# Dummy TensorE instructions ahead of three steps of the first batch

## The chip, the cores and the metric

The kernel runs on one core of a Trainium2 chip. The metric is device time in microseconds (us). A core has five engines that work side by side and wait for each other through semaphores: TensorE (PE in the profile, its weight loads are PEld), VectorE (DVE), ScalarE (ACT), GpSimd (POOL) and SyncE (SP, which here only issues DMAs). PSUM is the memory that TensorE writes its results into; DVE and ACT copy them from there to SBUF.

## What is computed

A cosformer attention without a softmax (features are a relu, weighted by a cosine and a sine of the position) is followed by an MLP mixer, with 8 batches, 8 heads, 576 positions and head dimension 64:

```python
def phi(x, c, s):
    r = np.maximum(x, 0.0)
    return np.concatenate([r * c, r * s], axis=-1)
q_p = phi(q, cos_w, sin_w)
k_p = phi(k, cos_w, sin_w)
kv = np.einsum('bhsf,bhsd->bhfd', k_p, v)
z = np.sum(k_p, axis=2)
num = np.einsum('bhsf,bhfd->bhsd', q_p, kv)
den = np.einsum('bhsf,bhf->bhs', q_p, z)[..., None] + 1e-06
x = num / den                     # heads side by side: (8, 576, 512)
...
xt = x.transpose(0, 2, 1)
h = np.maximum(xt @ w_tok1, 0.0) @ w_tok2
u = x + h.transpose(0, 2, 1)
h2 = np.maximum(u @ w_ch1, 0.0) @ w_ch2
return u + h2
```

## The kernel before

All 576 positions of a batch lie as five groups of rows on 128 partitions (index j from 0 to 4; P5 in the code pairs them as (0, 1), (2, 3) and (4,)). Heads come in two halves g = 0 and 1 of four heads each; g = 2 means all eight. The products are bf16 with sums in f32.

The order of the first two batches, and of part of the third and fourth, is written out as the string PLAN: each word is one step, called in that order, so that each engine receives its instructions in the order of the words. `turn.0.0.1` means batch 0, method `turn`, arguments 0 and 1. Engines run ahead of each other as far as the semaphores let them. From batch 2 on the loop `channel` runs the channel MLP of one batch with the attention of the next as hooks in between.

The steps of the first batch that the change and the prediction touch:

- `keep_warm` (L188 to L191) comes first on TensorE: 20 products of the zero tile with itself into a PSUM tile `wm`.
- `mkid` makes the 128x128 identity `ident` on GpSimd (masks.py in the trace).
- `feat` (L293) makes the features qp and kp from the loaded q and k, one group of rows, one half (cosine or sine) at a time, on ACT (L300) or DVE (L302).
- `cast` (L304) copies v to bf16 (`vbf`); the words that end in P run on GpSimd, whose queue also issues weight loads (`wt1`, `wt2`, `wu`, `wd`) and q of the second batch (`ldp`).
- `turn` (L309) transposes qp on TensorE, four heads for each group of rows, into a bf16 PSUM tile `tr`; `turno` copies that to `qpT` on ACT or DVE (L263, the line of all copies).
- `kvm` (L337) sums kp times v over the five groups into a PSUM tile `kv`, 20 products of 128x65 for one half of the heads; `kvo` copies it to SBUF.
- `num` (L368) multiplies qpT by kv, `numo` divides and writes `x` (DVE, L381 and L387).
- `w2a` copies the second token weights into their place (ACT, L263).
- `mix` (L403) multiplies the first token weights by x, into the PSUM tile `b1`.

Two PSUM pools serve them: psM, four slots of one bank, and psA, two slots of two banks. In the first batch `tr`, the kv tiles of half the heads and `b1` of half the heads are in psM. A step that takes a slot waits until the slot's last user is done with it.

A transpose and a product are both MATMUL instructions in the trace, each with a weight load of its own; L315 is the transposes' line, L331 that of the kv products, L361 and L365 those of num, L410 that of mix.

## Time and profile before

| | |
|---|---|
| median of 4 runs | 276.33 us (276.04 to 277.12) |
| profiled execution, its own time | 277.12 us |
| its span in the trace | 275.4 us, 4673 instructions |
| TensorE busy | 260.2 us, 94% of the span |
| DVE, ACT, POOL busy | 170.8, 116.5, 54.0 us |
| mean granted TensorE clock | 0.988 |
| idle TensorE ahead of the first transposes (L315, at 12.38 us) | 3.60 us, released by DVE qp |
| idle TensorE ahead of the next 24 (at 15.98 us) | 3.20 us, released by ACT qp |
| idle TensorE ahead of the first mix product (L410, at 22.01 us) | 1.12 us, released by DVE x |

The profile gives, for every instruction, its start and duration, and what ended the idle time of its engine before it. The granted clock is the share of TensorE's full clock that the chip allowed at that moment. Durations of matmuls are modelled and overlap, so the rate of a group is read from the starts of neighbouring groups. The chain that ended last is followed backwards from the last instruction, at each step to what released it, and shows which work set the end.

### The profile page before, as it was taken

The page shows a single profiled execution, that of the slowest core. Times are in us where ns is not written, and L with a number is a line of the kernel's source. Part 1 is how long each engine was busy: PE and PEld are TensorE (multiplying, and loading weights), DVE is VectorE, ACT ScalarE, POOL GpSimd, SP SyncE. Part 2 cuts the span into 40 slices and gives each one's busy share as a digit, 9 for nine tenths or more (in the row PEclk, how much of TensorE's full clock was granted, in tenths as well). Part 3 has the DMA queues.
Part 4 walks back from the last instruction along what each step waited for, and adds up shares of the span by engine and source line. Part 5 has one row for each costly group of instructions (what it writes and reads, how often), then busy time and mean ns, then how long its engine had stood idle before and what let it go on. Part 6 is the DMA issues. An engine that isn't in the chain of part 4 may idle for free.

```text
span 275.4 us, 4673 instructions
## 1 busy us (share of the span) xinstructions
PE 260.2 (94%) x1846; PEld 134.2 (49%) x1846; DVE 170.8 (62%) x338; ACT 116.5 (42%) x185; POOL 54.0 (20%) x76
## 2 busy tenths in 40 slices
PE   6367999999999999999999999999999999999994
PEld 2166556445544554454445544554455444444443
DVE  6467897599783476947584859485738543323322
ACT  2388684473790339133822482248224201301300
POOL 9580150051030005410160017001100120000000
PEclk9959999999999999999999999999999999999999
DMA  5999999999899999999999878930990073003012
GB/s 186 344 253 222 326 161 265 368 327 173 270 200 233 288 366 369 178 197 267 360 191 255 279 249 110 228 105 1 154 258 11 0 115 135 0 14 141 0 45 108
DMA packets 76005, 53.35 MB, mean 194 GB/s; under 512 B 47824, under 2 KB 72400, under 8 KB 75984
## 3 DMA queue, kind: packets, MB, share of 16 engines
q1 hardware_dynamic: 70256, 44.05, 61.5%
q0 software_dynamic: 5328, 8.49, 13.7%
q10 hardware_dynamic: 400, 0.52, 0.5%
q8 instruction: 14, 0.23, 0.3%
q14 instruction: 7, 0.06, 0.1%
HBM read 35.85 MB, written 9.44 MB: 164 GB/s over the span
## 4 chain that ended last, share of the span: by engine, by line
PE 87%; DMA 5%; ACT 3%; DVE 2%; POOL 1%; issue 1%; DVEq 0%; POOLq 0%; ACTq 0%
PE o_ps L583 25%; PE c_ps L566 25%; PE c L489 8%; PE o L501 6%; PE b L410 6%; PE u L437 5%; PE kv L331 3%; DMA kt<-in_k_dram 3%; PE nf L361 3%; PE tr L315 2%; DMA qpT<-qp 2%; PE ut L465 1%; ACT w L263 1%; PE o_ps L575 1%; ACT qp L300 1%; PE nm L361 1%
## 5 line engine op out<-in xcount | busy, mean ns | idle before, releaser
L267 ACT ACTIVATE h<-c_ps 128x512 bf16<-128x512 f32 x52 | 31.0, 597 | 109.7 <-PE c_ps L566 64.9
L583 PE MATMUL o_ps<-wc,h 128*128 128x512 bf16 x324 | 71.9, 379 | 0.0
L566 PE MATMUL c_ps<-uT,wc 128*128 128x512 bf16 x288 | 70.4, 379 | 0.0
L583 PEld LDWEIGHTS <-h 128*128 128x128 bf16 x324 | 31.7, 98 | 38.2
L566 PEld LDWEIGHTS <-wc 128*128 128x128 bf16 x336 | 30.8, 98 | 32.6
L269 DVE TENSOR_SCALAR h<-c_ps 128x512 bf16<-128x512 f32 x32 | 22.0, 688 | 28.4 <-PE c_ps L566 28.4
L263 POOL CAST ub<-u 128x1024 bf16<-128x1024 f32 x14 | 14.9, 1063 | 124.1 <-DVE u L442 83.7
L586 DVE TENSOR_TENSOR u<-o_ps,u 128x512 f32<-128x512 f32 x24 | 16.5, 688 | 17.6 <-PE o_ps L583 17.5
L263 POOL CAST vbf<-vt 128x512 bf16<-128x512 f32 (+3 forms) x28 | 20.3, 758 | 25.4 <-DMA vt<-in_v_dram 25.4
L300 ACT ACTIVATE qp<-qt,sin_t 128x512 bf16<-128x512 f32 x33 | 23.2, 711 | 2.3 <-DMA qt<-in_q_dram 2.3
L489 PE MATMUL c<-uT,wc 128*128 128x512 bf16 x96 | 23.3, 379 | 0.5 <-DVE u L513 0.5
L300 ACT ACTIVATE qp<-qt,cos_t 128x512 bf16<-128x512 f32 x32 | 22.6, 712 | 0.0
L501 PE MATMUL o<-wc,h 128*128 128x512 bf16 x96 | 22.2, 379 | 0.0
L387 DVE TENSOR_TENSOR x<-nf,den 128x512 bf16<-128x512 f32 x30 | 20.7, 691 | 1.0
L410 PE MATMUL b<-x,w 128*128 128x512 bf16 (+1 forms) x90 | 20.3, 355 | 1.1 <-DVE x L387 1.1
L442 DVE TENSOR_TENSOR u<-u,x 128x1024 f32<-128x1024 f32 x16 | 19.4, 1220 | 1.7 <-PE u L437 1.6
L361 PEld LDWEIGHTS <-qpT 128*128 128x128 bf16 x320 | 15.0, 98 | 9.5 <-DMA qpT<-qp 1.0
L302 DVE TENSOR_SCALAR kp<-kt,cos_t 128x512 bf16<-128x512 f32 x30 | 17.6, 588 | 2.4 <-DMA kt<-in_k_dram 2.4
L302 DVE TENSOR_SCALAR kp<-kt,sin_t 128x512 bf16<-128x512 f32 x30 | 16.5, 556 | 0.0
L383 DVE TENSOR_SCALAR den<-nf 128x8 f32<-128x8 f32 x30 | 5.0, 166 | 18.5 <-PE nf L361 18.4
L437 PE MATMUL u<-B,w 128*128 128x512 bf16 x64 | 16.3, 379 | 0.0
L501 PEld LDWEIGHTS <-h 128*128 128x128 bf16 x96 | 9.1, 97 | 10.4
(93 smaller groups left out, 252.7 us busy)
## 6 DMA issues: line engine op xcount, KB each, us to landing
out_dram<-u SPq DMA_DIRECT2D x32, 256.0 KB, 2.6
kt<-in_k_dram SPq DMA_DIRECT2D x7, 640.0 KB, 7.4
qt<-in_q_dram SPq DMA_DIRECT2D x6, 640.0 KB, 8.6
vt<-in_v_dram SPq DMA_DIRECT2D x6, 640.0 KB, 9.9
kt<-in_k_dram SPq DMA_DIRECT2D x7, 512.0 KB, 5.0
qt<-in_q_dram SPq DMA_DIRECT2D x6, 512.0 KB, 7.5
vt<-in_v_dram SPq DMA_DIRECT2D x6, 512.0 KB, 8.1
wc<-in_moe_w_ch_dram POOLq DMA_DIRECT2D x4, 384.0 KB, 8.4
```

Of the source, the lines that this page charges most:

```text
L263: (nc.scalar.copy if eng == "A" else ENG[eng].tensor_copy)(dst, src)
L267: nc.scalar.activation(dst, src, AF.Relu)
L269: nc.vector.tensor_relu(dst, src)
L300: nc.scalar.activation(dst, src, AF.Relu, scale=tab)
L302: ENG[eng].tensor_scalar(dst, src, scalar1=tab, scalar2=0.0, op0=ALU.mult, op1=ALU.max)
L361: nc.tensor.matmul(nm[:, hh * (D + 1):(hh + 1) * (D + 1)], self.qpT[:, j * H + h, :], self.kv[:, h, :D + 1], start=(not eps or hh == 0), s ...
L410: nc.tensor.matmul(b1[:, mi], w1[:, col(self.c, j), mi * P:(mi + 1) * P], self.x[:, j, cs], start=(j == 0 and (g == 2 or mi == 0)), stop=( ...
L437: nc.tensor.matmul(ps[:, jj], w2[:, ki, 1 + 2 * g + jj, :], self.B1[:, ki, :], start=(ki == 0), stop=(ki == NT - 1))
L489: nc.tensor.matmul(ps, wc1[:, ki, mi * P:(mi + 1) * P], self.uT[:, :, ki, :], start=(ki == 0), stop=(ki == NCC - 1))
L501: nc.tensor.matmul(self.ps["o", j], self.h1[:, ki, j * P:(j + 1) * P], wc2[:, ki, :], start=(ki == 0), stop=(ki == NCH - 1))
L566: nc.tensor.matmul(c_ps, wc1[:, ki, mi * P:(mi + 1) * P], uT[:, :, ki, :], start=(ki == 0), stop=(ki == NCC - 1))
L583: nc.tensor.matmul(o_ps, h1[:, ki, j * P:(j + 1) * P], wc2[:, ki, :], start=(ki == 0), stop=(ki == NCH - 1))
```

## The change

Three words are put into the plan, and nothing is taken out or moved: `warm.0.tr.0.1.73` ahead of `turn.0.0.1`, `warm.0.kv.0.0.2` ahead of `kvm.0.0`, `warm.0.b1.0.0.4` ahead of `mix.0.0.0`. The new method `warm` takes the PSUM tile which the following step will write, through the new method `place`, and issues a number of instructions with the zero tile as input into it: transposes of 128x128 for `tr`, else products of 128x512. The step that follows overwrites the tile. `turn`, `kvm`, `num`, `mix` and `ux` now get their tiles from `place` too, with the pools and shapes that they had.

```diff
+feat.0.q.4.2.0.D feat.0.k.4.2.0.D feat.0.q.0.2.1.D feat.0.q.1.2.0.A warm.0.tr.0.1.73 turn.0.0.1
...
+warm.0.kv.0.0.2 kvm.0.0 kvo.0.0.A cast.0.3.2.1.P kvm.0.1 num.0.0.0 turno.0.0.1.D numo.0.0.0 w2a.0.A
+warm.0.b1.0.0.4 mix.0.0.0 turno.0.1.0.A num.0.1.0 w2a.1.A turn.0.1.1 num.0.2.0 kvo.0.1.D num.0.0.1 numo.0.1.0
...
+        def place(self, kind, i, g):
+            pool = psM if self.b == 0 else psA
+            if kind == "tr":
+                return self.psum(("tr", i, g), psM, [P, 2, HH, P], BF16)
+            if kind == "kv":
+                return self.psum(("kv", g), psA, [P, 2, 512]) if g == 2 else self.psum(("kv", g), pool, [P, 512])
...
+            if kind == "b1":
+                return self.psum(("b1", g), psA if g == 2 else psM, [P, NT, Dm if g == 2 else Dm // 2])
...
+        def warm(self, kind, i, g, n):
+            t = self.place(kind, i, g)
+            for _ in range(n):
+                if kind == "tr":
+                    nc.tensor.transpose(t[:, 0, 0, :], zero[:, :P], ident)
+                else:
+                    if kind == "kv":
+                        o = t if g < 2 else t[:, 0]
...
+                    elif kind == "b1":
+                        o = t[:, 0] if g == 2 else t.rearrange("p n c -> p (n c)")
...
+                    nc.tensor.matmul(o, zero[:, :P], zero, start=True, stop=True)
...
-            tr = self.psum(("tr", i, g), psM, [P, 2, HH, P], BF16)
+            tr = self.place("tr", i, g)
...
-            if g == 2:
-                b1 = self.psum(("b1", g), psA, [P, NT, Dm])
-            else:
-                b1 = self.psum(("b1", g), psM, [P, NT, Dm // 2])
+            b1 = self.place("b1", 0, g)
```

## The prediction

> **What bounds the kernel now.** I read the busy shares by slice first.

> ```profile
> PE 260.2 (94%) x1846; PEld 134.2 (49%) x1846; DVE 170.8 (62%) x338; ACT 116.5 (42%) x185; POOL 54.0 (20%) x76
> PE   6367999999999999999999999999999999999994
> PEclk9959999999999999999999999999999999999999
> ```

> TensorE bounds the kernel from the fifth slice to the last. Only the first three slices (6.9 us each) have room on it, and in the third the granted clock is halved. The change acts there, so the next view is the table of stretches.

> ```profile
> 10.00:13.00 3.00, 0.40 (x4) 0.23 (x4) 1.41 (x3) 1.47 (x3) 1.53 (x2) 1.00 1.04 360
> 13.00:16.00 3.00, 0.02 (x1) 0.03 (x2) 2.84 (x4) 3.00 (x6) 2.81 (x4) 0.54 1.10 212
> 16.00:19.00 3.00, 3.00 (x33) 3.00 (x34) 2.05 (x4) 2.65 (x4) 3.00 (x5) 0.50 1.42 205
> 19.00:22.00 3.00, 1.89 (x45) 1.81 (x43) 1.03 (x3) 2.14 (x3) 0.45 (x1) 0.82 1.04 377
> 22.00:25.00 3.00, 2.75 (x53) 2.18 (x53) 2.12 (x7) 3.00 (x4) 0.00 (x0) 1.00 1.23 210
> ```

> In steps of 0.05 us, where the clock changes:

> ```profile
> 13.20:13.25 0.05, 0.00 (x0) 0.00 (x0) 0.05 (x1) 0.05 (x1) 0.05 (x1) 0.77 1.63 308
> 20.05:20.10 0.05, 0.05 (x6) 0.05 (x4) 0.00 (x0) 0.05 (x1) 0.00 (x0) 0.96 0.30 102
> ```

> The first two numbers are the stretch and its length, then come the busy times of PE, PEld, DVE, ACT and POOL, then the granted clock. TensorE is idle around 10 to 16 us. Its clock falls to 0.50 inside 13.20 to 13.25 (0.77 there puts it near 13.23) and is back at 1.00 inside 20.05 to 20.10 (0.96, near 20.05): a half-clock spell of 6.8 us. In the timeline:

> ```profile
> 2.27 6.51 PE L191 MATMUL wm<-zero 128*128 128x512 bf16 x20 [2.27 <-DVE zero L126]
> 12.38 0.40 PE L315 MATMUL tr<-ident,qp 128*128 128x128 bf16 x4 [3.60 <-DVE qp L302]
> 15.98 2.74 PE L315 MATMUL tr<-ident,qp 128*128 128x128 bf16 x24 [3.20 <-ACT qp L300]
> 17.05 0.58 ACT L263 COPY qpT<-tr 128x512 bf16<-128x512 bf16 x1
> 17.91 1.01 ACT L263 COPY qpT<-tr 128x1024 bf16<-128x1024 bf16 x1 [0.27 <-PE tr L315]
> 18.51 2.09 PE L331 MATMUL kv<-vbf,kp 128*128 128x65 bf16 x40
> 18.83 0.62 POOL L263 CAST vbf<-vt 128x512 bf16<-128x512 f32 x1
> 19.86 0.38 ACT L263 CAST kv<-kv 128x260 bf16<-128x260 f32 x1 [0.94 <-PE kv L331]
> 22.01 0.38 PE L410 MATMUL b<-x,w 128*128 128x256 bf16 x2 [1.12 <-DVE x L387]
> ```

> The 24 transposes and all 40 kv products fall in the spell. Last, the chain of waits says what that costs:

> ```profile
> 15.98 2.74 PE tr L315 x24
> 18.72 1.11 PE kv L331 x20
> 19.88 0.25 issue
> 20.13 1.38 ACT w L263
> 21.51 0.91 ACT qpT L263
> 22.42 1.29 ACT w L263
> ```

> From 15.98 to 19.83 the chain runs through half-clock TensorE. It then goes through ScalarE (copy of kv, two weight copies, two qpT copies) and returns to TensorE at 24.68. After that TensorE is nearly gapless; the waits of PE list 0.5 us for DVE (64.85) and 0.5 us for a DMA (125.79).

> **Part 1: 73 dummy transposes ahead of turn.0.0.1.** They need the zero tile (written by 2.2) and ident, whose POOL write starts at 8.79 and takes 0.35, so they start at about 9.2, behind the warm-up products. At full clock 8 transposes take 0.45 us (the x8 group at 31.20, its successor at 31.65), 56 ns each: 73 x 56 = 4.1 us, ending near 13.3. Queued behind them are only turn.0.0.1's first four transposes, which move from 12.38 to 13.3. Nobody notices, because the next four wait until 15.98 for qp from ACT. Were they all at half clock (24 in 2.53 us from 15.98 to 18.51, 105 ns each, 7.7 us in all), they would end at 16.9, 0.9 late; but the clock is 1.00 until 13.2, so that cover holds. Their PSUM tile is the one turn.0.0.1 writes, so no other tile waits. Time on the path: nothing.

> What they buy is the clock. Before it fell, TensorE had 0.4 us of work between 10 and 13. Now it has work until 13.5 and a gap of 2.5 us up to 15.98. I take it that this work counts and keeps the clock at 1.00. The other ways are the rivals.

> [...]

> At full clock the 24 transposes take 24 x 56 = 1.3 us and end issuing at 17.3 instead of 18.5.

> **Part 2: two 128x512 products ahead of kvm.0.0.** At full clock one takes 0.216 us (four take 0.86 in the chain). They and kvm.0.0 use a psM slot; four slots hold the four turned tiles, and the one freed first is the ACT copy 17.05 + 0.58 = 17.63. ACT is busy with kp until then whatever TensorE does. So they run 17.7 to 18.1, of which about 0.4 lies on the path. At half clock (the warm-up weight loads are 0.43 apart) they cost 0.85.

> The 20 products of kvm.0.0 at full clock: 40 take 1.27 us in the second batch (the group at 43.37), 32 ns each, 0.64 us: issue ends 18.76, results at about 18.92 (0.16 for the tail). Before it was 19.83. ACT's copy of kv then starts at 18.97, not 19.86, and ACT is free: its qpT copy, released by TensorE at 17.91 before, now follows the first at 17.55 and ends at 18.56. **Gain on ACT's chain: 0.89 us.** kvm.0.1 gains less: its last eight products need the POOL cast 18.83 + 0.62 = 19.45, so it ends at 19.76 instead of 20.45.

> **Part 3: four 128x512 products ahead of mix.0.0.0.** num.0.0.0 moves with kvm.0.1 by 0.69; it ends issuing at 20.05, and x, which mix.0.0.0 waits for, comes at 21.3 instead of 22.0. The four take 0.86 and fit into the 1.12 us idle that the row at 22.01 shows. Price zero; without that cover 0.86. At half clock, 1.7 us, they would stick out by 0.6. Mix then starts at 21.3, num.0.1.0 at 21.6 (its ACT copy ends 22.42 - 0.89), and turn.0.1.1 is done at 22.5, before ACT wants it at 22.7. So ACT's chain stays the limit and returns to TensorE at 23.8 instead of 24.68.

> **Does 0.89 us reach the end?** TensorE is the bound behind it, and the loads are early: for q of batch two ACT waits 2.3 us, until 54.54, and ACT has 1.7 us of idle afterwards (61.76), so that fixed date doesn't reach TensorE. The DVE stretch from 58.29 begins with a wait for TensorE and moves along. I pass it on in full; half lost to such dates would be 0.45.

> **Sum.** +0 (transposes) - 0.89 (clock, net of part 2) + 0 (part 3) = -0.89 us. The profiled execution took 277.12 us with a span of 275.4; it would become 276.2. The median of the runs shown is 276.33, 0.79 below the profiled one. Against it: 276.33 - 0.89 = **275.4 us**.

> **Rivals.**
> (a) Transposes don't feed the gate: slower. The clock falls at 13.23 as before. The transposes end at 18.51 as before, then the two dummies at half clock push kvm.0.0 by 0.85 to 19.36; with the clock back at 20.06 its 13 done and 7 x 32 ns left end at 20.29 instead of 19.55: +0.74 on ACT's chain, 277.1 us. From 0.5 (only kvm.0.1's shift counts) to 1.4 (0.85 in full and part 3 sticking out 0.6). It decides as soon as the spell still covers 17 to 19 us. For: there is no row of transposes alone. Against: the clock rose at 20.05 after a stretch of which transposes were a good half.
> (b) The spell comes one window later. Halving the 6.8 us of the spell, and stepping 3.4 from its start, the next judgement is at 16.65; from 13.24 to 16.65 TensorE has 0.9 us of work, 27%. Before the drop at 13.23 it had about 0.4 in the same length, and with 2.2 of 3.4 (6.4 to 9.8) it stayed up; 27% lies between. Then 12 transposes run fast and 12 slow (17.9), the dummies slow (18.8), kvm.0.0 ends at 19.81 instead of 19.55: +0.3, 276.6 us.
> (c) The profiled run had a costlier spell than the others. They are 0.64 to 1.08 us shorter, which a spell ending earlier would also give; then less is to be won, and the two dummies eat part of it: 0 to -0.5, 276.1 us. For: the spread of 1.08 us. Against: profiling alone may explain the one high run.

> **How the numbers follow.** A measurement of this kernel tells 0.3%, 0.83 us, from no change. Forecast 0.48, (a) 0.24, (b) 0.14, (c) 0.14. The forecast's own range is 274.9 to 275.9: further down if the half-clock spell of the usual run reaches beyond 20.05 (each 0.1 us of it costs 0.05), up to the half passed on. Of its 0.48, 0.38 lies under 275.50; (c) adds 0.04, where the usual run's spell is no shorter than thought: faster 0.42. Of (a)'s 0.24, 0.14 lies above 277.16 (its price runs from 0.5 to 1.4, most of that above 0.83), of (b) 0.04: slower 0.18. The rest, 0.40, is within. The range reaches from the forecast's lower end into (a)'s upper half: 274.9 to 277.2.

> **What would show it.** Right: granted clock 1.00 from 13.2 to 22, 24 transposes in about 1.3 us from 15.98, ACT's kv copy near 19.0, the num products that waited at 24.68 near 23.8, TensorE at 100 us ahead by 0.9. Wrong: a granted clock of 0.50 anywhere from 15.98 to 19; dummies past 15.98; mix.0.0.0 released by the dummies rather than by x; a new wait for a DMA between 25 and 70 us that swallows the lead.

## The result: slower by a quarter of a per cent, and the profile after

The changed kernel takes 277.11 us in the median of 53 runs (276.0 to 278.48), the kernel before 276.43 us in the median of 79. The ratio is 1.0025, with a 95% interval of 1.0017 to 1.0033: +0.7 us where -0.9 was forecast.

The profiled execution misleads at first sight: 276.26 us with a span of 274.4, one of the shortest of its kernel. Its first view, the busy shares and slices:

```profile
PE 264.5 (96%) x1925; PEld 137.3 (50%) x1925; DVE 171.1 (62%) x338; ACT 116.4 (42%) x185; POOL 54.1 (20%) x76
PE   6969999999999999999999999999999999999994
PEclk9999999999999999999999999999999999999999
```

TensorE has 79 products more, and the half-clock slice is gone. The table of stretches of the same execution (stretch, its length, busy PE, PEld, DVE, ACT, POOL, then granted clock, DMA share and GB/s):

```profile
10.00:13.00 3.00, 3.00 (x58) 3.00 (x55) 1.77 (x5) 1.99 (x4) 1.34 (x3) 1.00 1.03 357
13.00:16.00 3.00, 1.43 (x26) 1.26 (x24) 3.00 (x5) 3.00 (x6) 3.00 (x5) 1.00 1.12 219
16.00:19.00 3.00, 2.39 (x51) 2.03 (x49) 1.53 (x3) 2.16 (x5) 2.93 (x4) 1.00 1.39 198
19.00:22.00 3.00, 2.52 (x45) 1.61 (x42) 1.26 (x4) 3.00 (x4) 0.00 (x0) 1.00 1.07 379
22.00:25.00 3.00, 2.82 (x55) 2.38 (x52) 2.86 (x8) 2.10 (x3) 0.00 (x0) 1.00 1.21 209
```

So in this run, with the 73 transposes, the granted clock was 1.00 in all of these stretches. The timeline of TensorE, and ACT's copy of kv:

```profile
9.43 4.24 PE L311 MATMUL tr<-ident,zero 128*128 128x128 bf16 x73
15.46 1.51 PE L345 MATMUL tr<-ident,qp 128*128 128x128 bf16 x24 [1.57 <-ACT qp L330]
17.58 0.59 PE L321 MATMUL kv<-zero 128*128 128x512 bf16 x2 [0.61 <-DVE qpT L264]
18.85 0.38 ACT L264 CAST kv<-kv 128x260 bf16<-128x260 f32 x1 [0.84 <-PE kv L361]
19.59 1.02 PE L321 MATMUL b<-zero 128*128 128x512 bf16 x4
23.67 0.30 PE L390 MATMUL nm<-kv,qpT 128*128 128x65 bf16 x4 [0.16 <-ACT qpT L264]
```

The start of the 24 transposes depends on when q and k have landed, and that scatters from run to run (15.26 to 16.54 us in the traces of this study). I therefore split each trace in two: the **stage** from that start to the num products that wait for ACT's last qpT copy (15.98 to 24.68 before, 15.46 to 23.67 here), and the **rest** up to the end of the span (which is given to 0.1 us, so the rest is no finer). The stage fell from 8.70 to 8.21 us, a gain of 0.49; another 0.52 of this run's lead over the profiled run of before is only the earlier start. The rest is 250.7 us in both.

That makes two questions: why the median is slower when this trace is not, and where the other 0.4 of the forecast 0.89 went.

### The profile page after: what moved, and what is told of

Same layout as the page of the kernel before. It is cut to its first block, busy times and chain, and to the rows that moved or that the text cites. A ratio compares the mean times of both kernels' runs of the same rounds, so it can differ in the third digit from the quotient of the medians.

```text
span 274.4 us, 4831 instructions
## 1 busy us (share of the span) xinstructions
PE 264.5 (96%) x1925; PEld 137.3 (50%) x1925; DVE 171.1 (62%) x338; ACT 116.4 (42%) x185; POOL 54.1 (20%) x76
## 4 chain that ended last, share of the span: by engine, by line
PE 86%; DMA 5%; DVE 4%; ACT 2%; POOL 2%; issue 1%; DVEq 0%; POOLq 0%
PE o_ps L606 25%; PE c_ps L589 25%; PE c L512 8%; PE o L524 6%; PE b L433 6%; PE u L460 5%; PE nf L390 3%; DMA vt<-in_v_dram 3%; PE kv L361 3%; DMA qpT<-qp 2%; DVE qp L332 1%; PE ut L488 1%; ACT w L264 1%; PE o_ps L598 1%; DVE kp L332 1%; PE tr L345 1%
## 5 line engine op out<-in xcount | busy, mean ns | idle before, releaser
L332 DVE TENSOR_SCALAR kp<-kt,cos_t 128x512 bf16<-128x512 f32 x30 | 17.7, 591 | 2.2 <-DMA kt<-in_k_dram 2.2
L332 DVE TENSOR_SCALAR kp<-kt,sin_t 128x512 bf16<-128x512 f32 x30 | 17.3, 582 | 0.0
L409 DVE TENSOR_SCALAR den<-nf 128x8 f32<-128x8 f32 x30 | 5.0, 166 | 18.6 <-PE nf L390 18.5
(98 smaller groups left out, 260.2 us busy)
```

Source lines behind the costliest of these rows:

```text
L332: ENG[eng].tensor_scalar(dst, src, scalar1=tab, scalar2=0.0, op0=ALU.mult, op1=ALU.max)
```

## The experiments

Times are medians. The ratios stand against runs of the kernel before on the same chip, whose medians were 276.34 to 276.47; they are not the quotients of the two medians. The mean granted clock is listed for every run: about 0.994 is one half-clock spell of 3.4 us (e12's trace), 0.988 is one of 6.8 us (the trace of before). Values just below these and just below 1 are counted as no further spell: in the trace of the change the clock falls only at the end, inside 274.25 to 274.30 of a span of 274.4. "With a spell" below means a clock under 0.9955. "The gate" of the prediction and the expectations is whatever sets the granted clock.

**e1, e16: the kernel before, for the clock of its runs.**

> The kernel before, unchanged, for the granted clock of every run. Theory P (the phase of the clock gate differs from run to run, and the profiled run of before had one of the costliest spells): mean clocks spread from about 0.988 to 0.995 (half-clock spells of 6.8 down to 3.4 us, the shorter in at least half of the runs), the runs at 0.988 above 276.8 us, those at 0.993 and more below 276.4. Rival D (dummies simply cost their time on the path, the clock is the same in every run): all runs at 0.987 to 0.989, and the spread of 1 us has nothing to do with the clock.

276.67 us (ratio 1.001, 0.9997 to 1.0024). All 12 runs had clocks of 0.985 to 0.988; of the 140 runs of before that stand beside the experiments, 135 did not exceed 0.988. The length of the spell is the same whether a run takes 275.8 or 277.3 us, so theory P as I had put it fell for the kernel before. The trace has its spell from 14.97 to 21.80 instead of 13.23 to 20.05, and the stage takes 8.77 us.

**e2, e10: the 73 transposes alone.**

```diff
-warm.0.kv.0.0.2 kvm.0.0
+kvm.0.0
...
-warm.0.b1.0.0.4 mix.0.0.0
+mix.0.0.0
```

> Only the 73 transposes, without the two and the four 128x512 dummies. Theory P: two groups of runs as in the changed kernel, about half at a clock of 0.998 and more and about 276.2 us (the changed kernel's 276.6 less the 0.43 of the two dummies), the rest at 0.992 to 0.995 and about 276.9 (277.7 less 0.85): median 276.5. Rival D: the transposes do nothing to the time, the median is that of before, 276.4, and the clock is that of before in every run.

> The 73 transposes alone once more, beside the run with products: 276.9 to 277.4 under F and N, runs with a spell about 0.5 above those without it. If it comes out at 276.3 or less, the earlier 277.3 was scatter of twelve runs and both fall.

277.32 us (1.0041, 1.0017 to 1.0065) and 277.42 (1.0046, 1.0028 to 1.0064). In 15 of the 24 runs there was a spell (median 277.70), in 9 none (277.15). In e2's trace it runs from 16.23 to 19.65: 3.42 us, half as long as before. The stages of the two traces, 8.50 and 8.26 us, are shorter than before, and yet the kernel is 0.9 to 1.1 us slower. Neither P nor D has that.

**e3: the two and the four products alone.**

```diff
-warm.0.tr.0.1.73 turn.0.0.1
+turn.0.0.1
```

> Only the two and the four 128x512 dummies, without the transposes. Theory P: the spells are those of before, the two dummies cost 0.43 to 0.85 on the path, the four stick out in runs whose spell reaches 20 us: 277.0 to 277.4, clocks as before. Rival D: 277.1, the changed kernel's time, since the transposes do nothing.

277.24 us (1.0023, 1.0010 to 1.0036), clocks as before. Its trace has a stage of 9.56 us, 0.86 more than the profiled run of before: the two dummies at half clock, as large as two of the warm-up's half-clock products (0.85).

**e4: 108 transposes, no other dummies.**

```diff
-warm.0.tr.0.1.73 turn.0.0.1
+warm.0.tr.0.1.108 turn.0.0.1
```

(and without the other two words)

> 108 transposes instead of 73 and no other dummies: 108 x 56 ns = 6.0 us from 9.2 to 9.4 us, to about 15.4, so that no gap over 0.6 us is left ahead of the 24 transposes. Theory P (the gap from 13.5 to 15.9 is what lets the clock fall in half of the runs of the changed kernel): clock 0.998 and more in nearly all runs, one group of times around 276.0. Rival D: as with 73, 276.4. Rival N (transposes feed the gate too little): clocks of 0.992 to 0.995 in as many runs as with 73, or more.

275.85 us (0.9980, 0.9969 to 0.9991): no spell in any of 12 runs. Its table of stretches, with nothing but dummy transposes on TensorE:

```profile
11.00:12.00 1.00, 1.00 (x22) 1.00 (x19) 0.58 (x2) 0.49 (x1) 0.31 (x1) 1.00 1.00 358
13.00:14.00 1.00, 1.00 (x21) 1.00 (x19) 0.86 (x2) 1.00 (x3) 0.82 (x1) 1.00 1.04 255
```

With nothing but dummy transposes on TensorE for 6 us the clock stayed at 1.00. So N fell, and with the gap that the 73 leave closed no run lost the clock (0.997 to 1.000).

**e5, e12: the change again.**

> The changed kernel, unchanged, to see a run with a half-clock spell. Theory P2 (the gate judges fixed stretches of 3.41 us: it drops the clock after one with TensorE busy for less than about 40%, and raises it after one busy for more than about 77%): about half of the runs have a spell of 3.4 us, which starts between 15.5 and 24 us, in a run at 277.2 and more; the runs without it are at 276.0 to 277.1. Rival D (dummies cost their time, the clock doesn't matter): times of the runs don't go with their clocks.

> The changed kernel once more, for a trace with a spell and for more runs beside the others: 277.1, half of the runs at 0.992 to 0.994 and about 277.7, the rest at about 276.6. In a run with a spell it starts between 16 and 17 us, the two dummies take 0.85 and the four up to 1.7.

277.1 and 276.59 us (1.0027, 1.0009 to 1.0045; 1.0019, 1.0003 to 1.0035). Over all 75 runs of the change 35 had a spell (median 277.65) and 40 had none (276.51). e5's trace has none, with a stage of 8.22 us. e12's has one, from 17.01 to 20.42. The stretches and the timeline of e12:

```profile
16.00:19.00 3.00, 2.54 (x31) 1.82 (x29) 1.85 (x3) 2.33 (x4) 3.00 (x5) 0.67 1.40 198
19.00:22.00 3.00, 3.00 (x53) 2.41 (x51) 0.76 (x2) 1.95 (x3) 0.25 (x1) 0.76 1.07 379
```

```profile
17.90 1.01 PE L321 MATMUL kv<-zero 128*128 128x512 bf16 x2 [0.46 <-DVE qpT L264]
18.71 2.17 PE L361 MATMUL kv<-vbf,kp 128*128 128x65 bf16 x40
21.02 1.02 PE L321 MATMUL b<-zero 128*128 128x512 bf16 x4
```

The two dummies take 0.81 from start to start instead of 0.43, the 40 kv products 2.0 instead of 1.3. The four run at full clock again and lie in idle time. The stage is 9.09 us, 0.39 more than in the profiled run of before.

**e6, e7: the change without the four, and without the two.**

```diff
-warm.0.b1.0.0.4 mix.0.0.0
+mix.0.0.0
```

> The change without the four dummies ahead of mix.0.0.0. Theory P2: the wait for x ahead of mix (1.1 us) adds to the wait ahead of kvm, so more stretches between 17 and 24 us fall under 40%: more than half of the runs with a spell of 3.4 us, median 277.2 to 277.7. Rival D: the four lay in idle time, so nothing changes: 277.1.

```diff
-warm.0.kv.0.0.2 kvm.0.0
+kvm.0.0
```

> The change without the two dummies ahead of kvm.0.0. Theory P2: runs without a spell gain the 0.43 of the two dummies (about 276.2), about half still have a spell (277.2): median 276.7. Rival D: 277.1 less 0.43, 276.7, in all runs alike, whatever the clock.

277.32 us (1.0028, 1.0004 to 1.0051; 4 of 12 with a spell) and 276.89 (1.0013, 0.9996 to 1.0029; 6 of 12). Without the four dummies the spells did not become more, so P2's forecast for e6 (more than half of the runs) did not come true. Twelve runs can't tell 277.3 or 276.9 from the change's 277.1.

**e8, e9: the same 4.1 us filled with 19 long products, and with 73 short ones.**

```diff
-WARM = 20
+WARM = 39
```

> The kernel before with 39 instead of 20 warm-up products: 19 more 128x512 products at 0.216 us fill the same 4.1 us as the 73 transposes, without transposes. Theory P2 (products and transposes count alike): spells as in the run with 73 transposes alone (8 of 12 at 0.992 to 0.994), median 276.9 to 277.4. Rival N (transposes count less than products): clearly fewer spells than that, and a median of 276.2 or less.

```diff
+    def wms(n):
+        for i in range(n):
+            nc.tensor.matmul(wm0[:, :P], ident, zero[:, :P], start=True, stop=True)
...
-feat.0.q.1.2.0.A turn.0.0.1
+feat.0.q.1.2.0.A wms.73 turn.0.0.1
```

> 73 products of 128x128 into the warm-up's tile at the place of the 73 transposes, no other dummies: the same number of instructions at the same time, but no transposes. Theory F (the 146 added instructions shift the fetches of TensorE's program, which then fall on loads and on the transposing DMAs of qpT): as with the 73 transposes, 276.9 to 277.3. Rival N (transposes as such are at fault): as with the 19 added warm-up products, 275.9 to 276.1. Both expect about half of the runs with a spell of 3.4 us.

275.92 us (0.9980, 0.9966 to 0.9994; 7 of 12 with a spell) against 277.14 (1.0036, 1.0017 to 1.0055; 5 of 12). 1.2 us lie between two fills that last equally long, and spells don't explain it: e8's runs **with** a spell (276.14) beat e9's **without** (277.25). Nor do transposes, since e9's dummies are products. What is left, besides the form and the place of the dummies, is 108 instructions (each dummy is a weight load and a MATMUL). Theory F was right here; what the time goes with can be seen behind the stage. The same product of the third batch behind the first two, before and after, in the timelines:

```profile
125.79 0.43 PE L361 MATMUL nf<-kv,qpT 128*128 128x65 bf16 x8 [0.51 <-DMA qpT<-qp]
```

```profile
124.89 0.43 PE L390 MATMUL nf<-kv,qpT 128*128 128x65 bf16 x8 [0.62 <-DMA qpT<-qp]
```

All nine traces with about 73 added transposes or products, or with 108, have this wait (0.2 to 0.8 us). The traces of e3, e8, e11, e13, e14 and e15 have none. The DMA view of the changed kernel from 121.5 to 124.5 us (40 slices of 0.075 us; q8 is the queue that the profile calls instruction):

```profile
DMA  9999999999999000000000100000008999999999
GB/s 208 218 215 222 212 222 222 440 195 218 177 130 41 0 0 0 0 0 0 3 7 7 10 10 7 10 10 10 7 14 181 283 297 283 294 294 247 270 283 253
q8 instruction: 1, 0.02, 2.0%
qpT<-qp SPq DMA_TRANSPOSE x2, 5.0
```

Among the transposing DMAs of qpT lies a single fetch of 16 KB, at 122.1 us. Some 0.4 us behind its start the traffic falls from some 215 GB/s to between 0 and 14, for 1.2 us. In e9's view of the same window the fetch lies at 122.7, and the traffic is at 0 to 14 GB/s from 123.2 to 124.4.

**e11, e15: longer warm-ups.**

```diff
-WARM = 20
+WARM = 48
```

> The kernel before with 48 instead of 20 warm-up products, 28 x 0.216 = 6.0 us more: TensorE works up to between 14.4 and 15.7 us, so that the gap ahead of the 24 transposes is under 1.5 us. Theory P2: no spell in any run, and the 0.5 us between runs with and without a spell is won in all: 275.4 to 275.7. Rival D: as with 39, 275.9.

> The kernel before with 44 warm-up products: 24 x 0.216 = 5.2 us more, so that TensorE works up to about 14 us and the gap is under 2 us, with 48 instructions more. Theories P2 and F: no spell in any run, the fetch near 113, no wait for qpT: 275.4 to 275.7, about 0.3% faster than before. Rival: as with 48, 276.2, where a wait for the weights of the second channel product came up near 46 us in the traced run.

With 48: 276.2 us (0.9998, 0.9983 to 1.0014), no spell, half of the runs near 275.7 and half at 276.6 and more. The trace, from the slowest of them, has a stage of 7.80 us and then a wait of 0.9 us for weights of the second channel product. Part of the loss lies outside the span: seven of the 12 runs take 1.97 to 2.75 us longer than their span (2.75 in the traced one), while nearly all other runs here take 1.7 to 1.9. This trace has a 15th fetch, at 276.7, behind the end of the span; whether the two belong together no run shows. With 44: 275.67 (0.9986, 0.9967 to 1.0005), one spell in 12, again two runs above 277; its trace (275.49) has no wait for qpT, but one of 0.5 us for DVE's u_tail at 39.82, and a rest of 250.7. The expected 275.4 to 275.7 held for the median of the second only; the late weights I can't explain.

**e13, e14: the number of instructions, or the place of the fetch.** e13 is the change with `WARM = 39` in place of its transposes, so 108 instructions fewer. e14 has 147 products of 128x64 in place of e9's 73, so 148 more.

> The change with its 73 transposes replaced by 19 more warm-up products of 128x512, the same 4.1 us with 108 instructions fewer; the two and the four dummies stay. Theory F (a fetch of TensorE's program at 117 to 124 us holds up the transposing DMA of qpT): the fetch lies near 113, no wait for qpT near 125, and 0.5 to 0.8 us less than the change: 276.3 to 276.6, half of the runs with a spell and 0.8 above the rest. Rival S (only the spells make the loss): 277.0.

```diff
-            nc.tensor.matmul(wm0[:, :P], ident, zero[:, :P], start=True, stop=True)
+            nc.tensor.matmul(wm0[:, :64], ident, zero[:, :64], start=True, stop=True)
...
-feat.0.q.1.2.0.A wms.73 turn.0.0.1
+feat.0.q.1.2.0.A wms.147 turn.0.0.1
```

> 147 products of 128x64 in place of the 73 transposes, no other dummies: at 30 ns about the same 4.4 us, with 294 instructions more than before instead of 146. A fetch brings 16384 bytes, and TensorE's 158 more instructions in the change brought one fetch more and moved each some 10 us forward, so I take 256 instructions a fetch; 294 is then 38 past a whole fetch, as with 19 warm-up products. Theory F: a fetch near 113, none in 117 to 124, no wait for qpT, 275.9 to 276.2. Rival C (the number of instructions as such costs): 277.3 and more.

> The kernel before once more, for a third trace. Theory F: the fetch lies at 115 to 118 us, at the edge of the qpT DMAs, so a run has the wait near 125 or not; a run at 276.4 or less has none, a run at 277 and more has it. Rival S: the wait goes with no time of the run.

e13: 276.55 us (1.0006, 0.9988 to 1.0023), although 10 of its 12 runs had a spell: 0.5 less than the change. e14: 275.78 (0.9977, 0.9961 to 0.9992), 1.4 less than with 73 products, with **more** instructions; one run in 12 had a spell. In the traces the fetch lies at 111.9 us (e13) and 112.0 (e14), and there is no wait for qpT. e14's row of the product that waited, and its DMA view, 121.5 to 124.5 us:

```profile
124.79 0.42 PE L366 MATMUL nf<-kv,qpT 128*128 128x65 bf16 x8
```

```profile
DMA  9999999999999999999999999995899999999999
q1 hardware_dynamic: 2455, 0.62, 109.7%
qpT<-qp SPq DMA_TRANSPOSE x2, 3.9
```

No fetch, no hole, 2455 packets instead of the change's 1579, and 3.9 us to landing instead of 5.0. C fell. e16's trace, of a run at 276.32, has its fetch at 117.9: no wait, and a rest of 250.1 us. The two traces of before at 277.12 and 277.25 have the wait and 250.7 and 250.9. F's claim that a fetch in 117 to 124 always brings the wait is too coarse: with the fetch at 117.1 and 118.1 (e1) there is a wait, with the one at 117.9 there is none. The rows of SyncE's issue of the first transposing DMA of qpT, in the profiled run of before and in e16:

```profile
116.43 3.14 SPq L324 DMA_TRANSPOSE qpT<-qp  x1
```

```profile
115.86 1.84 SPq L324 DMA_TRANSPOSE qpT<-qp  x1
```

Before, the fetch at 117.1 lies inside that issue, which takes 3.14 us; in e16 the fetch at 117.9 comes just behind it, and it takes 1.84.

The traces side by side (us; the rest is the span less the end of the stage):

| trace | its time | stage | spell in it | rest | wait for qpT | fetch at |
|---|---|---|---|---|---|---|
| before | 277.12 | 8.70 | yes | 250.7 | 0.5 | 117.1 |
| before, e1 | 277.25 | 8.77 | yes | 250.9 | 0.6 | 118.1 |
| before, e16 | 276.32 | 8.77 | yes | 250.1 | none | 117.9 |
| change | 276.26 | 8.21 | no | 250.7 | 0.6 | 122.1 |
| change, e5 | 277.04 | 8.22 | no | 250.9 | 0.7 | 122.9 |
| change, e12 | 277.46 | 9.09 | yes | 250.8 | 0.7 | 122.5 |
| 73 products, e9 | 276.87 | 8.24 | yes | 250.9 | 0.7 | 122.7 |
| 147 products, e14 | 276.11 | 8.52 | yes | 249.9 | none | 112.0 |
| change with 39, e13 | 275.75 | 8.19 | no | 250.0 | none | 111.9 |

## Why the prediction was wrong, point by point

**"I pass it on in full": the step that failed.** TensorE was taken to be gapless behind the stage, and the one wait for qpT at 125.79 was read as a date of its own. But with the 158 added instructions the fetches on q8 came at other times: 14 before, the first at 23.5 us, 15 after, the first at 16.0, and each of the first 14 came 7.4 to 15.8 us earlier. The prediction's signs of being wrong looked for a new wait for a DMA only between 25 and 70 us; this one lies at 125. In the change the fetch falls into the qpT DMAs of the third batch in every trace, and the rest is 250.7 to 250.9 us; without the wait it is 249.9 to 250.1. Only the trace of e16, whose time lies by the median of before, shows how before runs without it. How many runs of before do is not measured; if most do, the loss is 0.7 us. An estimate from the traces speaks for most: with a stage that starts at 15.85, the middle of the traces, and the 1.8 us by which a time exceeds its span, 15.85 + 8.75 + 250.1 + 1.8 gives 276.5 for before (median 276.43), and 15.85 + 8.65 + 250.8 + 1.8 gives 277.1 for the change (277.11), with 8.65 as the mean of its two kinds of stage. That the loss goes with the place of the fetch, and not with the number of instructions, is shown by e8 and e9, by e13 (the change's fill, 0.5 us less) and by e14; that the fetch itself holds up the DMAs is read from the order of events in two traces (the change and e9) and not shown apart from it. A fetch brings 16 KB: 14 make 0.23 MB before, 15 make 0.25 MB after. Which engine it is for no view says; if all 14 serve TensorE, its 1846 products and as many weight loads make some 260 instructions a fetch (an estimate). e14 agrees: with 294 instructions more than before its fetch lies at 112.0, where e13 with 50 more has it at 111.9. No wait in TensorE's lists is for a fetch; the waits in question are all for the transposing DMA of qpT (0.2 to 0.8 us).

**-0.89 in the stage: right in direction, mis-sized.** In runs without a spell the stage gained 0.49 (8.70 to 8.21). The missing 0.4 is one term, the PSUM slot that kvm.0.0 waits for. I took the one freed first, by ACT's copy of a turned tile. The row at 17.58 names DVE's qpT copy as the releaser (16.86 + 0.67 = 17.53), 0.43 later than ACT's first copy of that run (16.54 + 0.56 = 17.10):

```profile
16.54 0.56 ACT L264 COPY qpT<-tr 128x512 bf16<-128x512 bf16 x1
16.86 0.67 DVE L264 COPY qpT<-tr 128x1024 bf16<-128x1024 bf16 x1
```

In the plan the tile of turn.0.0.1 is the oldest of the four, and its copy, turno.0.0.1.D, is the DVE's; e4, e5, e11, e12, e13 and e15 show the same releaser. Before, this wait was hidden behind the transposes at half clock, which issued until 18.51, while DVE's copy ended at 17.38 + 0.67 = 18.05. The two dummies themselves cost what was forecast, 0.4: without them, and with the clock up, the stage is 7.80 us (e11).

**Rival (b) came true in 35 of 75 runs.** Its price for the stage was +0.3; e12 measured +0.39. The interpolation behind it (0.9 us of work in 3.4 lets the clock fall) agrees with the traces. The short spells lasted 3.42 (e2) and 3.41 us (e12), the long ones 6.82 (before) and 6.83 (e1). Counted in stretches of 3.41 us back or on from where each trace's clock changes, the clock fell behind stretches in which TensorE worked 0.40 (before), 1.29 (e12), 1.32 (e2) and up to 1.49 us (e14), and stayed behind 1.50 (e1), 1.51 (e5, e13) and all that had more. P2's "about 40%" is 1.36 us of 3.41, a little lower than that; its "about 77%", 2.63 us, lies between the 2.54 behind which the clock stayed down and the 2.87 behind which it rose. What the chip itself goes by no run shows. The two rows at the border, e14's ahead of its fall at 15.76 and e1's, which starts two such stretches ahead of its fall at 14.97 and left the clock up at 11.56:

```profile
12.34:15.76 3.42, 1.49 (x48) 1.32 (x44) 3.12 (x5) 3.42 (x7) 2.85 (x5) 1.00 1.08 241
```

```profile
8.15:11.56 3.41, 1.50 (x7) 0.49 (x5) 1.27 (x4) 0.16 (x1) 1.82 (x4) 1.00 1.03 365
```

The ends of products are modelled, so these numbers are good to some 0.1 us, not to 0.01. Behind the 73 transposes lies a gap of 1.6 to 2.9 us, and the first rise of the clock differed between the traces (5.0 us in e4, 8.2 in e1); I take it that this is why such a stretch comes up in one run and not in another. I gave it 0.14 and treated it as one state of the kernel; it is a share of the runs. Half of -0.5 and half of +0.4 leave about nothing of the stage's gain.

**The sum from the runs:** stage 8.65 against 8.75, so -0.1, and rest up to +0.7, which makes up to +0.6; measured +0.7. Of the 1.6 us between that and the forecast of -0.9, the later slot makes 0.4, the spells 0.4 (0.88 in 35 of 75 runs) and the fetch up to 0.7.

**Rival (a), transposes don't feed the gate, fell:** with nothing but transposes on TensorE from 9.43 to 15.46 us e4's clock stayed at 1.00, and none of its 12 runs had a spell. **Rival (c), a costlier spell in the profiled run, fell as put:** spells of before are equally long (0.988), and its high profiled run is one with the wait for qpT. I had seen that 277.12 lay 0.79 above the median and put it down to a spell or to profiling; it was the trace with the wait.

**Part 1** held: the 73 ended at 13.5, and nothing waited for them. **Part 3** held: mix.0.0.0 followed the four without being released by them (20.76 against 19.59 + 0.86 = 20.45 for the dummies), and e12 hid them as well.

**A version that beats both.** Filling the first gap so that the fetch stays clear, or nearly (108 transposes wait 0.2), is faster than before by some 0.2%: 147 short products 0.9977 (0.9961 to 0.9992), 39 long ones 0.9980 (0.9966 to 0.9994), 108 transposes 0.9980 (0.9969 to 0.9991).

**Open:** the 73 transposes alone (277.4) came out 0.3 above the full change (277.1), against what stages and rests say. And of the 1.4 us between 73 and 147 products (e9, e14) the rests of the traces account for 1.0 (250.9 against 249.9); more spells with 73 (5 of 12 against 1) don't give the remainder, since e9's runs with a spell are no slower than those without.

## What to carry to other kernels

Filler instructions were not free here although TensorE was idle: with them the instruction fetches came 7.4 to 15.8 us earlier, and the runs with a fetch among the transposing DMAs lost more behind the stage (a rest of 250.7 to 250.9 us against 249.9 to 250.1) than the filler won (0.49); compare fillers of the same length with different numbers of instructions. A filler that only shortens an idle stretch may leave the clock to chance: here 35 of 75 runs had a spell, and none of 12 with the stretch closed (e4). If the profiled execution lies well off the median, find that difference first, before any change is priced.
